# One sink transposition per pair instead of two, and later products of weights and values, in an attention and feed-forward kernel

## The chip, the cores and the metric

The kernel runs on one core of a Trainium2 chip. The metric is the device time of one execution in microseconds (us), as the median of several runs.

## The reference

What is computed is windowed attention with sinks, and behind it a feed-forward part. There are 4 batches, 8 heads, 768 tokens and 64 elements per head; a token sees the first 4 tokens (sinks) and the last 128.

```python
scores = scale * np.matmul(q, k.transpose(0, 1, 3, 2))
keep = is_sink | in_window
scores = np.where(keep, scores, -1000000000.0)
a = np.exp(scores - np.max(scores, axis=-1, keepdims=True))
a = a / (np.sum(a, axis=-1, keepdims=True) + 1e-09)
attn = np.matmul(a, v)                    # heads side by side: 3072 x 512
h = attn @ w_in                           # 512 -> 2048
g = h * np.clip(h + 3.0, 0.0, 6.0) / 6.0
out = g @ w_out                           # 2048 -> 512
```

## The kernel before

**Tiling.** A unit is 256 tokens of one batch (`u` = 0, 1, 2), and a pair is two heads of a unit (`p` = 0 to 3). That makes 48 pairs, listed in `pus`: first the 16 pairs of the four units with `u` = 0, then 32 pairs with `u` > 0, batch by batch. Only the latter have a separate block of sinks (16 key columns), since the first 256 tokens hold the sinks themselves. The first ten pairs are `plain` and use fp32 operands. All others split each operand into a high and a low part (`split_parts`, line 28) in the type fp32r, and multiply the parts.

**Steps of a pair.** `A_kq` and `A_v` load K, Q and V. `B_k` and `B_q` split K and Q, and copy the parts between partitions by DMA (`K`, `Q`, one buffer each). `C_score` computes the scores of one head `h` and one tile `t` of 128 tokens on TensorE, and VectorE adds the mask and finds the minimum (line 314). `C_soft`, after the second tile of a head, runs the exponential on ScalarE (336), the reciprocal on VectorE (339), an addition on GpSimd (344) and the normalization (322). For `u` > 0 and `h` = 1 it then splits the sink weights of both heads and both tiles into `ssc` on VectorE (351 to 354). `D_pt` transposes the weights of a head on TensorE (362), splits them on ScalarE and VectorE into `ph` and `pl`, and GpSimd masks these (380, 382). `D_snk` transposes the sink weights: two products of `ssc` with the identity (392), and one copy to `pz` (395). `E_av` multiplies values and weights of a head into `av` (431); its last product for `u` > 0 takes the split sink values `vs` and `pz`. `E_out`, after head 1, adds the two halves on ScalarE and VectorE (452, 453) and splits the result into `xh` and `xl`.

**Sink values.** `batch_loads` loads them once per batch, at step V of the round in which that batch's first pair with `u` = 1 comes to E: `raw_s` by DMA from `vsx`, then ScalarE and VectorE split it into `vs`. There is one buffer `vs`. It has 128 partitions, of which the load fills 64; GpSimd clears it once, ahead of the first load (195).

**Feed-forward part.** When the fourth pair of a unit has passed `E_av` of head 1, `slot_E` appends the unit's 34 steps to `queues`: 16 of the first layer (`ffn1`, 12 matmuls of 256 columns each, line 469), 16 of the second (`ffn2`, 6 matmuls of 512 columns, line 489), and two outputs (`ffn_out`), which have no matmul. `drain(n)` takes n steps from the queues. A step is held back until enough weights have been loaded; these come with the step W of the first pairs.

**Order.** Instructions are issued in the order that the loop over `s` writes. In round `s`, the string `ORDER` (line 566) names the steps: C and D are for pair `s - 1`, E for pair `s - 2`, B for pair `s`, and V and L load ahead. Each `-` takes one feed-forward step. The framework inserts the semaphores, and it may place an instruction ahead of others that have no buffer yet. All PSUM tiles share 8 banks. The lines that the change touches are 179, 190, 192 to 198, 351, 385 to 396, 427, 566 and the layout of `vsx` at 737.

Of the kernel before, what the change touches and what calls it, by code (L numbers as in the profile page):

```python
# [9 lines left out]
F32 = mybir.dt.float32  # L10
F32R = mybir.dt.float32r
# [7 lines left out]
P = 128  # L19
SK = 16  # L20
# [24 lines left out]
def attn_ffn_kernel(ctx: ExitStack, tc: tile.TileContext, qx, kx, vx, vfx, vsx, n_sink, window, w_in, w_out, out):  # L45
    nc = tc.nc
    B, NU, NP = qx.shape[0:3]
    NT, DM = out.shape
    NFP = w_in.shape[0]
    H, D, UT = 2 * NP, 64, 256  # L50
    S = NU * UT
# [5 lines left out]
    work = fast.enter_context(tc.tile_pool(name="work", bufs=2))  # L57
# [11 lines left out]
    ident_r = const.tile([P, P], F32R, name="ident_r")  # L69
# [45 lines left out]
    def bias_from(dst, keep, engine=nc.vector):  # L115
        engine.tensor_scalar(out=dst, in0=keep, scalar1=-1.0, scalar2=BIG, op0=ALU.add, op1=ALU.mult)
# [15 lines left out]
    def weng(which, at):  # L132
        return {"D": nc.vector, "P": nc.gpsimd, "A": nc.scalar}[which[at % len(which)]]
# [42 lines left out]

    ssc = work.tile([P, 2, P], F32R, name="ssc", bufs=1)
    sinks = {}  # L180

    def later_constants():

        bias_from(m_t0[:, 0:P], prev, nc.gpsimd)
        bias_from(m_t0[:, P:2 * P], own, nc.gpsimd)
        bias_from(m_t0[:, 2 * P:W2], snk[:, 0:SK], nc.gpsimd)
        nc.gpsimd.tensor_copy(out=m_t1[:, 0:P], in_=m_t0[:, 0:P])
        nc.gpsimd.tensor_copy(out=m_t1[:, P:P + SK], in_=m_t0[:, 2 * P:W2])
        nc.gpsimd.tensor_copy(out=m_t1[:, P + SK:W2], in_=m_t0[:, P:2 * P])
        nc.gpsimd.memset(ssc.bitcast(F32), 0.0)  # L190

    def batch_loads(b):
        if not sinks:
            sinks["v"] = work.tile([P, NP, 4 * D], F32R, tag="vs", name="vs", bufs=1)
            nc.gpsimd.memset(sinks["v"].bitcast(F32), 0.0)
        v4 = sinks["v"][0:4 * SK].rearrange("p a (h d) -> p a h d", h=4)
        raw_s = work.tile([P, NP, 2, D], F32, tag="gf", name="raw_s", bufs=2)[0:4 * SK]
        nc.sync.dma_start(out=raw_s, in_=vsx[b])
        split_parts(nc, v4[:, :, 0::2, :], v4[:, :, 1::2, :], raw_s, nc.scalar, nc.vector)

# [127 lines left out]
    def C_soft(s, h):  # L328
        b, u, p = pus[s]
        d = st_[s]  # L330
        nb, sm, rc = d["nb"], d["sm"], d["rc"]
        hs = slice(2 * h, 2 * h + 2)
        live = [(0, W2), (0, W2)] if u else [(0, P), (0, 2 * P)]
        for t in range(2):
            i, blk = 2 * h + t, cell(s, h, t, *live[t])
            d["exp"] = nc.scalar.activation(out=blk, in_=blk, func=AF.Exp, scale=-1.0,  # L336
                                            bias=nb[:, i:i + 1], accum_out=sm[:, i:i + 1])
        nc.vector.tensor_scalar(out=sm[:, hs], in0=sm[:, hs], scalar1=1e-9, scalar2=None, op0=ALU.add)
        nc.vector.reciprocal(out=rc[:, hs], in_=sm[:, hs])  # L339
        if u:  # L340

            both = d["P"][:, h].rearrange("p (t w) -> p t w", t=2)[:, :, P:2 * P]
            prior = d["P"][:, h, 0:2 * WP].rearrange("p (t w) -> p t w", t=2)[:, :, 0:P]
            nc.gpsimd.tensor_tensor(out=both, in0=both, in1=prior, op=ALU.add)  # L344
            live = [(P, W2), (P, W2)]
        for t in range(2):
            i, blk = 2 * h + t, cell(s, h, t, *live[t])
            norm((NORM0 if s < START else NORM)[i], blk, rc[:, i:i + 1])
        if u and h == 1:

            ss = ssc[:, :, 0:4 * SK].rearrange("p t (k h y) -> p t k h y", k=2, h=2)
            snk_in = d["P"][:, :, 2 * P:2 * WP].rearrange(
                "p h (t y) -> p t h y", t=2)[:, :, :, 0:SK]
            split_parts(nc, ss[:, :, 0], ss[:, :, 1], snk_in, weng(SSE, 0), weng(SSE, 1))
# [30 lines left out]
    def D_snk(s):  # L385
        b, u, p = pus[s]
        if not u:
            return
        d = st_[s]
        sp = ps.tile([P, 512], F32, tag="bank", name="spt")  # L390
        for t in range(2):
            nc.tensor.matmul(out=sp[:, t * P:(t + 1) * P], lhsT=ssc[:, t, :],
                             rhs=ident_r, start=True, stop=True)
        pz = work.tile([P, UT], F32R, name="pz", bufs=1)
        nc.scalar.copy(out=pz, in_=sp[:, 0:UT])
        d["pz"] = pz

    def E_av(s, h):
        b, u, p = pus[s]
        d = st_[s]  # L400
        VS = d["VS"]
        if h == 0:
            d["av"] = ps.tile([P, 2, UT], F32, tag="bank", name="av")
            if not plain(s):
                d["tmp"] = work.tile([P, UT], F32, name="tmp", bufs=1)
        acc = d["av"][:, h, :]

        if u:
            ops = [(1, P, 0, UT), (0, 0, 0, P), (2, 3 * P, P, UT)]
        else:  # L410
            ops = [(0, 0, 0, UT), (1, 2 * P, P, UT)]
        if plain(s):
            pf = d[f"pt{h}"]
            seq = [(VS[:, slot, h, :], pf[:, c:c + o1 - o0], d["av"][:, 0, o0:o1]) for slot, c, o0, o1 in ops]
        else:

            ph, pl = d[f"pt{h}"]
            vsl = slice(2 * D * h, 2 * D * (h + 1))
            vhi = slice(2 * D * h, 2 * D * h + D)
            high = [(VS[:, slot, vsl], ph[:, c:c + o1 - o0], acc[:, o0:o1]) for slot, c, o0, o1 in ops]  # L420
            low = [(VS[:, slot, vhi], pl[:, c:c + o1 - o0], acc[0:D, o0:o1]) for slot, c, o0, o1 in ops]
            seq = [high[0]]
            for a, l in zip(high[1:], low[1:]):
                seq += [a, l]

            if u:
                seq += [low[0], (sinks["v"][:, p, vsl], d["pz"], acc)]
            else:
                seq.append((VS[:, 0, vsl], pl[:, 0:UT], acc))
        for j, (l, r, o) in enumerate(seq):  # L430
            nc.tensor.matmul(out=o, lhsT=l, rhs=r, start=(j == 0 and (h == 0 or not plain(s))),  # L431
                             stop=(j == len(seq) - 1 and (h == 1 or not plain(s))))
        if h == 1:
            E_out(s)
# [128 lines left out]
                dsts = [out[r0 + P * tt:r0 + P * (tt + 1), :] for tt in range(2)]  # L563
                queues.append(ffn_steps(units.index((b, u)), xt[(b, u)], work, ps, ps, dsts, "bank"))

    ORDER = "V C00 - C01 E0 - C10 - C11 E1 L - Bk - Bq W - D0 - S D1 -"
    MULT = [1] * 12
    WN = [0, 1, 1, 1, 1, 4, 4, 4, 4, 4, 4, 4]

    for s in range(NS + 2):  # L570
        if s == 3:
            later_constants()
        for step in ORDER.split():
            if step == "-":
# [43 lines left out]
    with tc.If(flag == 1):  # L618
        with ExitStack() as gen:
# [71 lines left out]
            with tc.For_i(0, B, 1) as bi:  # L691
                for u in range(NU):
                    xn = gp.tile([P, NP, UT], F32, name="xn")
                    for c in range(NP):
                        nc.sync.dma_start(out=xn[:, c, :],
                                          in_=xv[ds(bi, 1), :, c, u * UT:(u + 1) * UT].rearrange("o p s -> (o p) s"))
# [12 lines left out]
def _layout(q, k, v, n_sink, window, moe_w_in, moe_w_out):  # L709

    import numpy as _np

    B, H, S, D = q.shape
    NU, NP, T = S // 256, H // 2, 128
    qT = q.reshape(B, NP, 2, S, D).transpose(0, 1, 2, 4, 3).reshape(B, NP, T, S)
    kT = k.reshape(B, NP, 2, S, D).transpose(0, 1, 2, 4, 3).reshape(B, NP, T, S)
    vp = v.reshape(B, NP, 2, S, D).transpose(0, 1, 3, 2, 4)
    qx = _np.zeros((B, NU, NP, T, 256), q.dtype)
    kx = _np.zeros((B, NU, NP, T, 400), k.dtype)
    vx = _np.zeros((B, NU, NP, T, 3, 2, D), v.dtype)  # L720
    for u in range(NU):
        qx[:, u] = qT[..., 256 * u:256 * (u + 1)]
        if u:
            at = [range(256 * u - T, 256 * u + T), range(16), range(256 * u + T, 256 * (u + 1))]
            tiles = range(2 * u - 1, 2 * u + 2)
        else:
            at = [range(256)]
            tiles = range(2)
        at = [j for r in at for j in r]
        kx[:, u, :, :, 0:len(at)] = kT[..., at]  # L730
        for j, t in enumerate(tiles):
            vx[:, u, :, :, j] = vp[:, :, T * t:T * (t + 1)]

    vfx = _np.zeros((B, NP, T, 2, 2, 2, D), v.dtype)
    for h in range(2):
        vfx[:, :, :, :, h, h] = vp[:, :, 0:2 * T, h].reshape(B, NP, 2, T, D).transpose(0, 1, 3, 2, 4)
    vsx = _np.zeros((B, 4, 16, NP, 2, D), v.dtype)
    for r in range(4):
        vsx[:, r, :, :, r % 2] = vp[:, :, 0:16, r % 2].transpose(0, 2, 1, 3)
    DM, DF = moe_w_in.shape  # L740
    w_in = moe_w_in.reshape(DM // T, T, DF // 256, 256).transpose(2, 1, 0, 3)
    w_out = moe_w_out.reshape(DF // 256, 2, T, DM).transpose(0, 2, 1, 3)
    return {'qx': qx, 'kx': kx, 'vx': vx,
            'vfx': vfx.reshape(B, NP, T, 2, 2, 2 * D),
            'vsx': vsx.reshape(B, 64, NP, 2, D), 'n_sink': n_sink, 'window': window, 'w_in': w_in, 'w_out': w_out}


# [24 lines left out]
```

## Time and profile before

| | us |
|---|---|
| median of 3 runs (lowest to highest) | 739.97 (739.43 to 742.04) |
| the profiled execution, its own time | 739.71 |
| its span, first to last instruction | 738.0 |
| TensorE matmuls busy | 715.6 |
| TensorE weight loads busy | 642.3 |
| VectorE busy | 509.2 |
| ScalarE busy | 423.3 |
| GpSimd busy | 172.6 |

The span is the profiled execution from its first to its last instruction. Busy times of an engine are added up over its instructions without overlap. Matmuls are pipelined, so their rows overlap, and TensorE's busy share says little about single ones. In the rows, PE is TensorE's matmul, PEld its weight load, DVE is VectorE, ACT is ScalarE, POOL is GpSimd, and SPq is the queue from which SyncE issues DMAs. L392 is line 392 of the kernel. `out<-in` names the tile written and the tiles read.

### The profile page before, as it was taken

How to read it: one execution, taken by the hardware profiler on the slowest of the kernel's cores; microseconds unless marked ns; L12 is line 12 of the kernel's file. 1: busy time of each engine (PE TensorE's matmuls, PEld its weight loads, DVE VectorE, ACT ScalarE, POOL GpSimd, SP SyncE). 2: the span in 40 equal slices, each digit the busy share in tenths (PEclk: the TensorE clock that was granted, in tenths of full speed). 3: DMA queues.
4: the chain of work that ended last, by engine and by line, in shares of the span. 5: the costliest groups of instructions: out<-in, count | busy, mean ns of one | idle time of the engine just before them, and what ended most of it. 6: DMA issues, size and time to landing. Idle time of an engine off the chain costs nothing.

```text
span 738.0 us, 14278 instructions
## 1 busy us (share of the span) xinstructions
PE 715.6 (97%) x4804; PEld 642.3 (87%) x4804; DVE 509.2 (69%) x1418; ACT 423.3 (57%) x1107; POOL 172.6 (23%) x337
## 2 busy tenths in 40 slices
PE   8899999999999999999999999999999999999996
PEld 7677788999989998989898989899889889998995
DVE  5798999666777767776866876866876775633321
ACT  5998987657556556556555555755655654411111
POOL 1000000000233533433433442343343343200000
PEclk9999999999999999999999999999999999999998
DMA  6657673535536436436435644643643632000000
GB/s 235 185 179 228 197 239 101 144 94 151 132 98 169 117 96 175 126 89 169 118 96 127 158 105 103 171 108 99 175 116 88 168 89 60 30 1 1 30 1 33
DMA packets 55345, 88.58 MB, mean 120 GB/s; under 512 B 8416, under 2 KB 38368, under 8 KB 55264
## 3 DMA queue, kind: packets, MB, share of 16 engines
q1 hardware_dynamic: 55120, 87.59, 43.8%
q8 instruction: 40, 0.66, 0.4%
q14 instruction: 41, 0.34, 0.1%
q10 hardware_dynamic: 144, 0.00, 0.0%
HBM read 41.95 MB, written 6.29 MB: 65 GB/s over the span
## 4 chain that ended last, share of the span: by engine, by line
PE 74%; DVE 8%; ACT 8%; DMA 4%; issue 3%; POOL 2%; SPq 1%; DVEq 0%; ACTq 0%; POOLq 0%
PE o L489 29%; PE hps L469 29%; PE av L431 6%; PE sp L312 4%; PE pt L362 2%; PE sp L307 2%; DMA st<-in_w_out_dram 1%; ACT Pt L336 1%; ACT Pt L322 1%; DMA st<-in_w_in_dram 1%; POOL Pt L344 1%; DVE Pt L314 1%; DVE tmp L453 1%; ACT Ph L336 1%; DVE xl L455 1%
## 5 line engine op out<-in xcount | busy, mean ns | idle before, releaser
L469 PE MATMUL hps<-xh,wih 128*128 128x256 f32 x768 | 220.4, 287 | 2.8 <-ACT wih L35 2.6
L469 PE MATMUL hps<-xh,wil 128*128 128x256 f32 x768 | 217.5, 283 | 0.1
L469 PE MATMUL hps<-xl,wih 128*128 128x256 f32 x768 | 216.3, 282 | 0.0
L489 PE MATMUL o<-woh,gh 128*128 128x512 f32 x384 | 155.7, 405 | 2.1 <-DVE gh L41 1.9
L489 PE MATMUL o<-woh,g 128*128 128x512 f32 x384 | 151.8, 397 | 0.6 <-DVE g L478 0.5
L489 PE MATMUL o<-wol,gh 128*128 128x512 f32 x384 | 151.3, 394 | 0.0
L469 PEld LDWEIGHTS hps<-xh,wih 128*128 128x128 f32 x768 | 144.7, 188 | 5.9 <-ACT wih L35 3.9
L469 PEld LDWEIGHTS hps<-xl,wih 128*128 128x128 f32 x768 | 144.7, 188 | 1.4
L469 PEld LDWEIGHTS hps<-xh,wil 128*128 128x128 f32 x768 | 144.5, 188 | 1.6 <-DVE wil L165 0.5
L336 ACT ACTIVATE Pt<-Pt,nb 128x272 f32<-128x272 f32 (+2 forms) x152 | 77.1, 508 | 73.4 <-DVE nb L314 71.8
L475 ACT ACTIVATE gf<-hps,three 128x512 f32<-128x512 f32 x96 | 65.8, 685 | 83.9 <-PE hps L469 83.0
L476 DVE SCALAR_TENSOR_TENSOR gf<-gf,hps 128x512 f32<-128x512 f32 x96 | 65.9, 686 | 67.3 <-ACT gf L475 66.3
L344 POOL TENSOR_TENSOR Pt<-Pt 128x256 f32<-128x256 f32 x64 | 47.9, 748 | 194.1 <-ACT Pt L336 194.1
L489 PEld LDWEIGHTS o<-woh,g 128*128 128x128 f32 x384 | 72.2, 188 | 19.7 <-DVE g L478 3.0
L322 ACT ACTIVATE Pt<-Pt,rc 128x144 f32<-128x144 f32 (+2 forms) x152 | 55.8, 415 | 54.0 <-DVE rc L339 32.4
L489 PEld LDWEIGHTS o<-woh,gh 128*128 128x128 f32 x384 | 72.3, 188 | 13.0 <-DVE gh L41 2.8
L314 DVE CUSTOM_DVE_ANT_0 Pt<-sp,m_t 128x272 f32<-128x272 f32 x128 | 54.5, 434 | 41.9 <-PE sp L312 41.8
L489 PEld LDWEIGHTS o<-wol,gh 128*128 128x128 f32 x384 | 72.5, 189 | 10.5
L478 DVE TENSOR_TENSOR g<-gf,gh 128x512 fp32r<-128x512 f32 x96 | 70.0, 729 | 1.2
L312 PE MATMUL sp<-K,Q 128*128 128x272 f32 (+2 forms) x304 | 61.0, 286 | 0.2 <-issue 0.2
L312 PEld LDWEIGHTS sp<-K,Q 128*128 128x128 f32 x304 | 51.3, 188 | 7.0 <-DMA Q<-qt 0.4
L380 POOL TENSOR_SCALAR_AFFINE_SELECT ph<-ph 128x256 fp32r<-128x256 f32 x64 | 29.8, 466 | 113.7 <-ACT ph L35 113.2
(97 smaller groups left out, 1111.2 us busy)
## 6 DMA issues: line engine op xcount, KB each, us to landing
K<-kt SPq DMA_DIRECT2D x128, 200.0 KB, 3.5
Q<-qt SPq DMA_DIRECT2D x152, 64.0 KB, 2.5
st<-in_w_in_dram SPq DMA_DIRECT2D x16, 512.0 KB, 4.3
st<-in_w_out_dram SPq DMA_DIRECT2D x16, 512.0 KB, 5.3
kr<-in_kx_dram SPq DMA_DIRECT2D x32, 200.0 KB, 2.5
qr<-in_qx_dram SPq DMA_DIRECT2D x48, 128.0 KB, 2.4
out_dram<-ost SPq DMA_DIRECT2D x24, 256.0 KB, 2.5
vr<-in_vx_dram SPq DMA_DIRECT2D x32, 192.0 KB, 2.6
```

Of the source, the lines that this page charges most:

```text
L312: nc.tensor.matmul(out=sp[:, 0:w], lhsT=Q[:, h, t * P:(t + 1) * P], rhs=K[:, h, part, k0c:k0c + w], start=(part == 0), stop=(part == 1))
L314: d["min"] = nc.vector.tensor_tensor_reduce(out=cell(s, h, t, 0, w), in0=sp[:, 0:w], in1=m[:, 0:w], scale=-SCALE, scalar=3.0e38, op0=ALU.a ...
L322: nc.scalar.mul(out=blk, in_=blk, mul=c)
L336: d["exp"] = nc.scalar.activation(out=blk, in_=blk, func=AF.Exp, scale=-1.0, bias=nb[:, i:i + 1], accum_out=sm[:, i:i + 1])
L344: nc.gpsimd.tensor_tensor(out=both, in0=both, in1=prior, op=ALU.add)
L380: nc.gpsimd.affine_select(out=prior[i], in_=own[i], pattern=[[0, 2], [-1, P]], base=0, channel_multiplier=1, compare_op=ALU.is_gt, fill=0.0)
L431: nc.tensor.matmul(out=o, lhsT=l, rhs=r, start=(j == 0 and (h == 0 or not plain(s))), stop=(j == len(seq) - 1 and (h == 1 or not plain(s))))
L469: nc.tensor.matmul(out=hp[:, half, :], lhsT=l, rhs=r, start=(j == 0), stop=(j == n - 1))
L475: nc.scalar.activation(out=gf, in_=hp, func=AF.Relu, bias=three, scale=1.0)
L476: nc.vector.scalar_tensor_tensor(out=gf, in0=gf, scalar=6.0, in1=hp, op0=ALU.min, op1=ALU.mult)
L478: eng(GLO, state["n"] * NP).tensor_tensor(out=g, in0=gf, in1=gh.bitcast(F32), op=ALU.subtract)
L489: nc.tensor.matmul(out=acc, lhsT=l[:, f, ts_], rhs=r[i][:, f, :], start=(i == 0 and f == 0 and j == 0), stop=(i == NFP - 1 and f == 1 and ...
```

## The change

`ssc` gets one tile of 128 columns, in which the parts, tiles and heads of the sink weights lie side by side, so one product with the identity transposes them all. Its result has the rows of tile 0 in partitions 0 to 63 and those of tile 1 in partitions 64 to 127. Two copies put the first into columns 0 to 127 of `pz`, and the second into columns 128 to 255; the rest of `pz` was cleared once and stays zero. `pz` is now one lasting tile. The sink values are laid out twice, in all 128 partitions, and `vs` isn't cleared any more. In `ORDER`, E0 moves from behind C01 to behind C11, E1 moves from behind C11 to behind Bk, and S moves behind D1. There are eight `-` in both orders.

```diff
-    ssc = work.tile([P, 2, P], F32R, name="ssc", bufs=1)
+    ssc = work.tile([P, P], F32R, name="ssc", bufs=1)
+    pz = work.tile([P, UT], F32R, name="pz", bufs=1)
...
-        nc.gpsimd.memset(ssc.bitcast(F32), 0.0)
+        nc.gpsimd.memset(pz.bitcast(F32), 0.0)
...
             sinks["v"] = work.tile([P, NP, 4 * D], F32R, tag="vs", name="vs", bufs=1)
-            nc.gpsimd.memset(sinks["v"].bitcast(F32), 0.0)
-        v4 = sinks["v"][0:4 * SK].rearrange("p a (h d) -> p a h d", h=4)
-        raw_s = work.tile([P, NP, 2, D], F32, tag="gf", name="raw_s", bufs=2)[0:4 * SK]
+        v4 = sinks["v"].rearrange("p a (h d) -> p a h d", h=4)
+        raw_s = work.tile([P, NP, 2, D], F32, tag="gf", name="raw_s", bufs=2)
...
-            ss = ssc[:, :, 0:4 * SK].rearrange("p t (k h y) -> p t k h y", k=2, h=2)
+            ss = ssc.rearrange("p (t k h y) -> p t k h y", t=2, k=2, h=2)
...
         sp = ps.tile([P, 512], F32, tag="bank", name="spt")
+        nc.tensor.matmul(out=sp[:, 0:P], lhsT=ssc, rhs=ident_r, start=True, stop=True)
         for t in range(2):
-            nc.tensor.matmul(out=sp[:, t * P:(t + 1) * P], lhsT=ssc[:, t, :],
-                             rhs=ident_r, start=True, stop=True)
-        pz = work.tile([P, UT], F32R, name="pz", bufs=1)
-        nc.scalar.copy(out=pz, in_=sp[:, 0:UT])
-        d["pz"] = pz
+            rows = slice(4 * SK * t, 4 * SK * (t + 1))
+            nc.scalar.copy(out=pz[rows, t * P:(t + 1) * P], in_=sp[rows, 0:P])
...
-                seq += [low[0], (sinks["v"][:, p, vsl], d["pz"], acc)]
+                seq += [low[0], (sinks["v"][:, p, vsl], pz, acc)]
...
-    ORDER = "V C00 - C01 E0 - C10 - C11 E1 L - Bk - Bq W - D0 - S D1 -"
+    ORDER = "V C00 - C01 - C10 - C11 E0 L - Bk E1 - Bq W - D0 - D1 S -"
...
-    vsx = _np.zeros((B, 4, 16, NP, 2, D), v.dtype)
-    for r in range(4):
+    vsx = _np.zeros((B, 8, 16, NP, 2, D), v.dtype)
+    for r in range(8):
         vsx[:, r, :, :, r % 2] = vp[:, :, 0:16, r % 2].transpose(0, 2, 1, 3)
```

## Rows read from the trace of the kernel before

**Rows 1.** The page: busy us (share of the span) and instructions.

```profile
PE 715.6 (97%) x4804; PEld 642.3 (87%) x4804; DVE 509.2 (69%) x1418; ACT 423.3 (57%) x1107; POOL 172.6 (23%) x337
```

**Rows 2.** Stretches: length, busy us (instructions) by engine, granted clock, DMA share, GB/s.

```profile
0.00:120.00 120.00, 112.13 (x670) 91.69 (x670) 100.23 (x298) 101.95 (x251) 3.09 (x16) 1.00 0.67 207
120.00:640.00 520.00, 512.23 (x3550) 468.16 (x3551) 378.01 (x1069) 306.63 (x834) 169.55 (x321) 1.00 0.46 119
```

**Rows 3.** Waits, 120 to 640 us: waiting line, releaser, us, times, longest.

```profile
PE av L431 <- DVE vs L30: 3.2, 4, 1.5
PE spt L392 <- DVE ssc L30: 1.6, 2, 1.2
PE o L489 <- DVE gh L41: 1.1, 1, 1.1
...
PE o L489 <- DVE g L478: 0.5, 1, 0.5
...
PEld av L431 <- DVE vs L30: 4.2, 4, 1.7
```

**Rows 4.** Line 392: minimum/median/maximum ns, first and last start in us.

```profile
L392 PEld LDWEIGHTS spt<-ident_r,ssc x64: 186/188/192, 199.5 to 633.8; 128*128 128x128 f32 x64
L392 PE MATMUL spt<-ident_r,ssc x64: 221/273/327, 199.7 to 633.8; 128*128 128x128 f32 x64
```

**Rows 5.** Chain of waits, 250 to 260 us: start, us, engine, tile, line, count.

```profile
251.88 1.43 PE hps L469 x12
...
254.97 0.17 PE spt L392 x2
255.14 0.25 PE pt L362 x2
255.39 1.40 PE o L489 x6
...
258.42 0.25 PE sp L312 x2
258.67 0.65 PE av L431 x7
```

**Rows 6.** Timeline at the fourth batch's sink values: start, us; idle before in brackets.

```profile
533.69 0.49 SPq L198 DMA_DIRECT2D raw_s<-in_vsx_dram  x1
...
538.25 0.85 DVE L30 TENSOR_TENSOR vs<-raw_s,vs 64x512 fp32r<-64x512 f32 x1 [1.26 <-ACT vs L35]
...
539.16 0.38 PE L431 MATMUL av<-pz,vs 128*128 128x256 f32 x1 [0.87 <-DVE vs L30]
```

**Rows 7.** DMA issues: count, KB each, median us to landing.

```profile
VF<-in_vfx_dram SPq DMA_DIRECT2D x10, 256.0 KB, 3.8
...
raw_s<-in_vsx_dram SPq DMA_DIRECT2D x4, 128.0 KB, 2.8
```

**Rows 8.** Groups by form, ScalarE: busy us, mean ns, idle before.

```profile
L452 ACT COPY tmp<-av 64x256 f32<-64x256 f32 x76 | 27.8, 366 | 23.5 <-DVE tmp L453 13.2 <-DVE xl L455 9.0
...
L395 ACT CAST pz<-spt 128x256 fp32r<-128x256 f32 x32 | 11.7, 366 | 4.0 <-PE spt L392 4.0
...
L336 ACT ACTIVATE Ph<-Ph,nb 128x256 f32<-128x256 f32 x20 | 10.0, 498 | 0.0
...
L336 ACT ACTIVATE Ph<-Ph,nb 128x128 f32<-128x128 f32 x20 | 7.9, 394 | 7.3 <-DVE nb L314 7.2
```

**Rows 9.** Waits of TensorE, 0 to 120 us.

```profile
PE pt L362 <- DVE Ph L324: 2.4, 3, 1.1
```

**Rows 10.** Timeline around 265 us, SP and TensorE; last row, Q's issues, us to landing.

```profile
265.15 3.02 SPq L275 DMA_DIRECT2D Q<-qt  x4
...
270.82 0.41 PE L312 MATMUL sp<-K,Q 128*128 128x272 f32 x2
...
Q<-qt SPq DMA_DIRECT2D x152, 64.0 KB, 2.5
```

**Rows 11.** Groups by form, VectorE, line 453.

```profile
L453 DVE TENSOR_TENSOR tmp<-av,tmp 64x256 f32<-64x256 f32 x76 | 31.9, 420 | 16.2 <-ACT tmp L452 15.7
```

More of the change, by code (lines that the diff above doesn't have):

```diff
@@ L744, in _layout @@
             'vfx': vfx.reshape(B, NP, T, 2, 2, 2 * D),
-            'vsx': vsx.reshape(B, 64, NP, 2, D), 'n_sink': n_sink, 'window': window, 'w_in': w_in, 'w_out': w_out}
+            'vsx': vsx.reshape(B, 128, NP, 2, D), 'n_sink': n_sink, 'window': window, 'w_in': w_in, 'w_out': w_out}
 def kernel(**inputs):
```

## Prediction

> **What bounds the kernel now.** I read the share of busy time first: TensorE's matmuls cover 97% of the span, its weight loads 87% [rows 1]. Such a share is an average, so I cut the span into stretches [rows 2]. Up to 120 us, while weights are loaded and the first tiles (plain fp32) run, VectorE and ScalarE are busy for 100.2 and 102.0 of 120 us and TensorE for 112.1. From 120 to 640 us, where the 32 pairs with sinks lie (sink transpositions from 199.5 to 633.8 us [rows 4]), TensorE is busy for 512.2 of 520 us, VectorE for 378.0 and ScalarE for 306.6. After 640 us only the feed-forward part is left. The granted clock is 1.00, 2.4 GHz, in the first two stretches. So between 120 and 640 us a matmul taken away is worth its place in the stream, and a wait of TensorE is worth its length; work of the other engines is free as long as it ends in time.
>
> Then I read whom TensorE waits for in that stretch [rows 3]: 3.2 us for `vs`, the split sink values (four waits, one per batch), 1.6 us for `ssc` (two), 1.6 us for `gh` and `g` of the feed-forward part. That is 6.4 of the 7.8 us by which TensorE falls short of 520.
>
> A matmul's own duration is no price, since matmuls overlap (the sink transpositions show a median of 273 ns [rows 4]). The price is what the chain of waits gives to a run of them [rows 5]: 12 feed-forward matmuls of 256 columns in 1.43 us, 119 ns each; two sink transpositions in 0.17 us, 85 ns each.
>
> **The sum, part by part.** *One transposition fewer.* Now each sink pair issues two 128x128 products with the identity, x64 [rows 4]; then one, x32. Each is worth 0.17/2 = 0.085 us; bounds are half of a 256-column slot, 0.06, and half of the 0.25 us that the two transpositions of D1 take behind them [rows 5], 0.12. I take 0.085, the row of the thing itself: 32 x 0.085 = 2.7 us (1.9 to 3.8). The Trainium skill, page "TensorE: Matmul & The Clock Gate", section "Wait — 56ns, not 53.3ns?", has a 128-column matmul at 55.6 ns in a warm stream; by it this term would be 1.8 us, an estimate from that page, and the sum 0.9 us smaller. The row is of the same instruction with its own weight load and decides.
>
> *Products of weights and values later.* E0 goes past C10, C11 and two feed-forward steps, E1 past the loads of the next pair (L), one step and Bk. Their last product reads `vs`, which is filled anew per batch. In the fourth batch the load is issued at 533.69, VectorE ends the split at 538.25 + 0.85 = 539.10, and the product starts at 539.16, 0.87 us late [rows 6]. In the new order it comes two steps (1.4 us each, as the 12 matmuls or the six wide ones of the second layer [rows 5]) and two scores (0.25 each, of two matmuls [rows 5]) later: 3.3 us. The longest wait [rows 3] is 1.5, so all four go. Worth: 3.2 us as TensorE's idle, 4.2 as the idle of its weight loads [rows 3]; I take 3.2 plus 4 x 0.1 for the product after the stall (0.38 against its usual 0.28 us), 3.6. What is late next is nothing of `vs`.
>
> *Sink rows doubled.* The load grows from 64 rows (128 KB) to 128 rows (256 KB). Rows at both ends: 2.8 us to land for 128 KB, 3.8 for the 256 KB of VF [rows 7], so up to 1.0 us more, four times; the nearest row in size is VF and I take the full 1.0. It is covered by the 3.3 - 1.5 = 1.8 us that are left; uncovered it would cost 4 us at most. The split keeps 512 elements per row, and a row count doesn't show in these durations: `tmp` with 64 rows of 256 takes as long as `pz` with 128 [rows 8]. GpSimd's clearing of `vs` goes; the clearing of `pz` replaces that of `ssc` (256 columns both). Neither is waited for.
>
> *Two copies for `pz` instead of one.* Now 128x256 in 0.366 us. No row shows 64x128. From below: 256 against 128 columns differ by 0.104 us for the exponentials [rows 8], so 0.26 each, 0.16 more per pair; from above: two full ones, 0.37 more. I take 0.16, since columns and not rows set it: 32 x 0.16 = 5 us of ScalarE, 12 at most, in a stretch where it has 213 us free [rows 2]. The copies now stand behind the evacuation of D1 on ScalarE, which that gains. Their reader is E0's last product, four steps later. Uncovered, it would be 0.16 per pair on the path. VectorE's split into `ssc` has the same 128x64 elements: nothing.
>
> *S behind D1, C11 ahead of E0.* Two pairs waited for `ssc`. C11 now runs 0.65 us (seven products of E0 [rows 5]) earlier and S 0.25 later, but D1 comes first and needs the normalized weights, ready 0.4 us before `ssc` (two VectorE splits). I take half of the 1.6 us, 0.8 (bounds 0 and 1.6).
>
> *First stretch.* Three waits of the transpositions for VectorE's normalizing, 2.4 us together [rows 9]; with C11 ahead of E0 they may shrink. But VectorE and ScalarE are 84% busy there [rows 2], converting weights. I take 0 (bounds 0 and 2.4). The feed-forward steps of the first unit begin one step later; they are held back by the count of loaded weights anyway.
>
> *Queues.* E issues no DMA, so SP's queue keeps its order. ScalarE's split of V waits for the buffer that E1 of two pairs before reads, now about 2 us later; its own reader comes two pairs later, so nothing. SP's K and Q copies of the next pair overwrite what C11 reads, so they go out behind it. In one pair Q's four go from 265.15 to 268.17, behind K's, land 2.5 us later at 270.7, and the next score starts at 270.82 [rows 10]. There is little room; but between C11 and the next pair's C00 there were five steps and one E, and will be five steps and two E, 0.65 us more. I cost this at nothing; 0.5 us late in each pair would be 16 us.
>
> Sum: 2.7 + 3.6 + 0.8 = 7.1 us. The profiled execution took 739.71 us (span 738.0 and 1.7 around it), 0.26 below the median: 739.97 - 7.1 = 732.9.
>
> **Rivals.** *The waits only move (0.15).* `vs` is ready in time, but TensorE, no longer stopped, meets the next late thing. For: 0.2 to 1.1 us waits for `gh`, `g` and `ssc` are there already [rows 3]. Against: VectorE has 27% free in this stretch [rows 2]. Then only the matmul pays: 739.7 - 2.7 = 737.0.
>
> *TensorE isn't the bound (0.08).* The Trainium skill, page "Perfetto Trace Analysis", section "Identifying the Most-Contended Engine", says to judge TensorE's headroom by weight loads, not by matmul busy time. As a mechanism here: the 13% without a weight load [rows 1] would be real room, the stream would be held by buffers or evacuations, and what is saved would turn into other gaps; the time stays 739.7. Against: six 512-column matmuls take 1.40 us, 233 ns each, back to back, while a weight load is 188 ns [rows 4, 5], so weight loads rest there with the array full.
>
> *Slower: VectorE's second half fills up (0.07).* E_out's VectorE operations (two sums of 0.42 us each [rows 11] and the two parts of x) move behind Bk, into the half pair that already has the splits of K, V, Q and of both D's. The feed-forward chain (gf, gh, g) queues behind them, and the second-layer product waits for `gh` or `g`, as it does once with 1.1 us [rows 3]. It decides from 7.1/32 = 0.22 us of new wait per pair; at 0.5 us it is 16 us against 7: 739.7 - 7.1 + 16 = 748.6. Against: VectorE is busy 73% [rows 2], and E_out ran into that half before too, a step and an E (2 us) earlier.
>
> **How the numbers follow.** Forecast 0.70, rivals 0.15, 0.08, 0.07. The likeliest gives 732.8. Its own ends: all low, 1.9 + 3.2 + 0 = 5.1, gives 734.9; all high, 3.8 + 4.2 + 1.6 + 2.4 = 12.0, gives 728.0. The range reaches to the first rival with 1.5 us beyond and leaves out the slower one: 728.5 to 738.5. About 0.5%, 3.7 us, is what a measurement can tell from no change, so faster means below 736.3: the forecast and a quarter of the first rival, 0.74; same 0.19; slower 0.07.
>
> **What would show it.** Right: x32 sink transpositions; TensorE's row for `vs` gone; TensorE idle from 120 to 640 us below 4 us; pz copies x64 near 0.26 us; K and Q landing before their scores. Wrong: a row of TensorE for `gh`, `g`, `pz` or Q of several us, an unchanged or larger idle sum, or a first stretch that takes longer.

## The result and the profile after

The changed kernel takes 731.26 us (median of 4 runs, 730.63 to 732.62) against 739.76 for the kernel before in the same job: a ratio of 0.988, 95% interval 0.986 to 0.990, 8.5 us less. The forecast was 732.8 us, range 728.5 to 738.5. The profiled execution took 730.63 us, span 728.9, which is 9.1 less than the span before.

The page and the stretches of the changed kernel, columns as in [rows 1, 2]:

```profile
PE 709.6 (97%) x4772; PEld 635.8 (87%) x4772; DVE 495.4 (68%) x1418; ACT 426.3 (58%) x1139; POOL 169.6 (23%) x336
```

```profile
0.00:120.00 120.00, 111.15 (x684) 91.76 (x685) 103.25 (x301) 104.56 (x257) 3.08 (x16) 1.00 0.66 210
120.00:640.00 520.00, 515.60 (x3571) 469.67 (x3570) 366.09 (x1075) 309.71 (x864) 166.54 (x320) 1.00 0.47 121
```

There are 32 matmuls fewer. From 120 to 640 us TensorE falls short by 4.4 us instead of 7.8 [rows 2]. In the first 120 us it has issued 684 matmuls instead of 670. Its waits from 120 to 640 us in the changed kernel are these (compare [rows 3]):

```profile
PE sp L312 <- DMA Q<-qt: 1.9, 3, 1.0
PE o L487 <- DVE gh L41: 1.4, 4, 0.5
PE o L487 <- DVE g L476: 0.4, 2, 0.2
```

The rows for `vs` and `ssc`, 4.8 us, are gone. A row for Q has come, 1.9 us. The instructions of `ssc`, `pz` and the sink values in the changed kernel (minimum/median/maximum ns, first and last start), and the DMA issues (columns as in [rows 7]):

```profile
L391 PE MATMUL spt<-ident_r,ssc x32: 305/306/308, 197.6 to 622.8; 128*128 128x128 f32 x32
...
L394 ACT CAST pz<-spt x64: 246/260/267, 198.2 to 623.6; 64x128 fp32r<-64x128 f32 x64
...
L35 ACT ACTIVATE vs<-raw_s x4: 615/634/635, 201.5 to 527.8; 128x512 fp32r<-128x512 f32 x4
```

```profile
VF<-in_vfx_dram SPq DMA_DIRECT2D x10, 256.0 KB, 3.6
...
raw_s<-in_vsx_dram SPq DMA_DIRECT2D x4, 256.0 KB, 2.9
```

A copy into half of `pz` takes 0.260 us. Twice the sink values land in 2.9 us, against 2.8 before [rows 7].

The chain of waits of the changed kernel around a sink transposition, columns as in [rows 5]:

```profile
250.36 1.43 PE hps L467 x12
251.79 0.22 PE pt L362 x2
252.01 0.06 PE spt L391
252.07 1.47 PE hps L467 x12
...
258.50 0.25 PE sp L312 x2
...
267.67 0.25 PE sp L312 x2
```

Before, the two sink products and D1's two transpositions took 0.17 + 0.25 = 0.42 us together [rows 5]. Now it is 0.22 + 0.06, and 0.04 more for the run behind them (1.47 us instead of 1.43): 0.32. So by this one pair a sink transposition is worth 0.10 us, and 32 of them 3.2 us.

### The profile page after: what moved, and what is told of

Read it like the earlier page. It is cut to its first block, busy times and chain, and to the rows that moved or that the text cites. A ratio compares the mean times of both kernels' runs of the same rounds, so it can differ in the third digit from the quotient of the medians.

```text
span 728.9 us, 14295 instructions
## 1 busy us (share of the span) xinstructions
PE 709.6 (97%) x4772; PEld 635.8 (87%) x4772; DVE 495.4 (68%) x1418; ACT 426.3 (58%) x1139; POOL 169.6 (23%) x336
## 4 chain that ended last, share of the span: by engine, by line
PE 79%; DVE 7%; ACT 5%; DMA 5%; issue 2%; SPq 1%; POOL 0%; ACTq 0%; DVEq 0%; POOLq 0%
PE hps L467 32%; PE o L487 31%; PE av L429 6%; PE sp L312 5%; PE pt L362 3%; DMA K<-kt 2%; PE sp L307 2%; SPq L262 1%; DMA Q<-qt 1%; DVE gf L474 1%; DVE g L476 1%; ACT Pt L336 1%; DMA st<-in_w_out_dram 1%; ACT gf L473 1%; PE idle L81 1%
## 5 line engine op out<-in xcount | busy, mean ns | idle before, releaser
L380 POOL TENSOR_SCALAR_AFFINE_SELECT ph<-ph 128x256 fp32r<-128x256 f32 x64 | 32.5, 512 | 155.7 <-ACT ph L35 155.7
```

The lines of the kernel that those rows point to most:

```text
L380: nc.gpsimd.affine_select(out=prior[i], in_=own[i], pattern=[[0, 2], [-1, P]], base=0, channel_multiplier=1, compare_op=ALU.is_gt, fill=0.0)
```

## The experiments

Each ratio is to the kernel before, run on the same chip in the same job, with a 95% interval. Three more measures come from the profiled execution, one of each kernel, without an interval. **The rest** runs from the issue of the first output DMA to the end of the span. It compares kernels of one order alone, because the first output stands at different places of TensorE's stream: behind 726 or 727 matmuls in the order of before (before, e1, e4, e8), 743 or 744 in the new one, 731 or 732 with E1 behind E0 in the first rounds (e6, e9, e12). **The middle** runs from the first score product of the first pair with sinks to that of the last pair. It holds the same steps of the pairs in every kernel, 31 of the 32 sink transpositions and all four waits for `vs`. **The end** is what follows. The two executions of the changed kernel agree in the middle to 0.02 us (424.75 and 424.77), those of e6 and e12 to 0.03.

| kernel | median us | ratio (interval) | first output at | the rest | the middle | the end |
|---|---|---|---|---|---|---|
| before | | 1 | 129.8 | 608.2 | 433.6 | 116.6 |
| changed | 731.26 | 0.988 (0.986 to 0.990) | 130.4 | 598.5 | 424.8 | 118.6 |
| e1 merge only | 738.02 | 0.995 (0.994 to 0.997) | 132.2 | 605.3 | 430.9 | 116.6 |
| e2 order only | 737.78 | 0.996 (0.994 to 0.998) | 132.6 | 602.5 | 428.5 | 118.9 |
| e3 second product | 734.97 | 0.991 (0.989 to 0.993) | 132.7 | 602.7 | 428.4 | 119.1 |
| e4 sinks once | 735.96 | 0.994 (0.992 to 0.996) | 130.0 | 604.3 | 429.7 | 116.6 |
| e5 S ahead of D1 | 730.39 | 0.987 (0.984 to 0.990) | 129.9 | 598.2 | 424.1 | 119.0 |
| e6 E1 behind E0 | 726.87 | 0.981 (0.979 to 0.983) | 126.4 | 598.1 | 424.3 | 116.7 |
| e7 output on ScalarE | 735.73 | 0.992 (0.989 to 0.994) | 136.7 | 603.1 | 429.4 | 117.7 |
| e8 first rounds old | 732.98 | 0.989 (0.987 to 0.992) | 130.7 | 601.4 | 426.6 | 116.7 |
| e9 E1 early in first rounds | 728.68 | 0.984 (0.982 to 0.987) | 127.5 | 599.3 | 426.2 | 116.0 |
| e10 E1 early in later rounds | 735.70 | 0.992 (0.989 to 0.994) | 129.6 | 603.7 | 429.6 | 118.8 |
| e11 changed again | 731.07 | 0.986 (0.984 to 0.989) | 129.9 | 598.5 | 424.8 | 118.5 |
| e12 E1 behind E0 again | 727.19 | 0.981 (0.978 to 0.983) | 128.6 | 598.0 | 424.4 | 116.6 |

The stretch ahead of the middle, the middle and the end, of the kernel before and then of the changed one, and behind them the middles of e2 and e3, columns as in [rows 2]; each middle goes from the start of one `sp` product to that of another:

```profile
0.00:187.80 187.80, 179.53 (x1128) 153.32 (x1129) 148.89 (x441) 145.70 (x369) 4.05 (x17) 1.00 0.59 175
187.80:621.39 433.59, 426.22 (x2971) 389.67 (x2969) 316.77 (x885) 254.60 (x693) 162.05 (x307) 1.00 0.49 124
621.39:738.00 116.61, 109.89 (x709) 99.30 (x707) 43.49 (x93) 23.02 (x45) 6.54 (x14) 0.98 0.04 15
```

```profile
0.00:185.56 185.56, 175.85 (x1117) 150.09 (x1117) 148.95 (x440) 145.39 (x369) 3.08 (x16) 1.00 0.59 176
185.56:610.31 424.75, 421.55 (x2945) 385.24 (x2943) 303.09 (x886) 257.19 (x724) 160.89 (x308) 1.00 0.50 129
610.31:728.90 118.59, 112.20 (x715) 100.48 (x713) 43.31 (x93) 23.73 (x47) 5.65 (x13) 1.00 0.04 15
```

```profile
187.75:616.22 428.47, 425.17 (x2976) 389.47 (x2974) 302.14 (x886) 249.48 (x692) 161.54 (x309) 1.00 0.49 126
187.90:616.26 428.36, 424.76 (x2975) 388.64 (x2974) 301.78 (x886) 254.20 (x723) 161.71 (x309) 1.00 0.50 127
```

**The merge alone (e1).** The changed kernel with the order of before:

```diff
-    ORDER = "V C00 - C01 - C10 - C11 E0 L - Bk E1 - Bq W - D0 - D1 S -"
+    ORDER = "V C00 - C01 E0 - C10 - C11 E1 L - Bk - Bq W - D0 - S D1 -"
```

> The changed kernel with the order of steps of before: one sink transposition, two copies for pz, sink values in 128 rows, E0 and S where they were. My theory: only the matmul term is earned, 32 x 0.085 = 2.7 us (up to 3.8), and the four waits of TensorE for vs stay (3 us or more): 736 to 737 us. Rival, the order is needed for nothing: 731.3 as the whole change. Rival, TensorE isn't the bound: 739.8, as before. If the doubled load of sink values made itself felt, the waits for vs would grow by up to 1.0 us each, and the time would be up to 4 us more, 740 to 741.

738.02 us, 0.995, or 3.5 us less (2.2 to 4.7); the rest is 2.9 us shorter, the middle 2.7. TensorE's waits from 120 to 640 us, first three rows:

```profile
PE av L429 <- DVE vs L30: 3.6, 4, 1.4
PE o L487 <- DVE gh L41: 1.5, 2, 1.2
PE spt L391 <- DVE ssc L30: 1.3, 2, 0.7
```

The matmul is earned, and the waits for `vs` stay, as the theory said. The doubled load lengthens them from 3.2 to 3.6 us, not by 1.0 us each.

**The order alone (e2).** The kernel before with the new `ORDER`:

> The kernel before with the new order of steps alone: two sink transpositions, one copy, sink values in 64 rows. My theory: the waits for vs go (3.6 us), those for ssc shrink or go (0.8 to 1.6), so 734.5 to 735.5 us, and TensorE's row for vs is empty. Rival, the waits only move: 739.8, with new rows for gh, g or Q of as many us. If the two parts are independent, the gains of this run and of the run with the order of before add up to the 8.5 us of the whole.

737.78 us, 3.2 us less (1.6 to 4.7): the sign is right, the size of the median below the forecast. TensorE's waits from 120 to 640 us have no row for `vs` or `ssc`:

```profile
PE o L489 <- DVE gh L41: 1.9, 4, 0.7
PE sp L312 <- DMA Q<-qt: 1.4, 2, 0.8
PE o L489 <- DVE g L478: 0.2, 1, 0.2
```

The middle is 5.1 us shorter; the forecast for these waits was 4.4. The end is 2.3 us longer (see E1 below). Most of the scatter goes with the clock. Four of e2's twelve executions had a mean granted clock of 0.997 or more and took 734.5 to 735.7 us, about as forecast; seven at 0.990 to 0.994 took 737.3 to 740.9. The kernel before took 739.1 to 741.6 us in twelve executions at 0.998 or 0.999, and 742.0 to 744.1 in nine at 0.993 or 0.994. In the profiled execution of e2 the clock fell in the first stretch, at a wait of 2.2 us for a weight:

```profile
60.00:65.00 5.00, 2.79 (x14) 2.13 (x12) 4.20 (x14) 4.37 (x13) 0.00 (x0) 0.90 0.41 118
65.00:70.00 5.00, 5.00 (x24) 3.81 (x23) 4.45 (x13) 4.46 (x10) 0.00 (x0) 0.76 0.70 233
```

With e1 the two parts give 3.5 + 3.2 = 6.7 us by the runs, against 8.5 to 8.8 for the whole, and 2.7 + 5.1 = 7.8 against 8.8 by the middle. Within the intervals the parts add up. The missing 1.0 us is about what TensorE's waits grew in e1 (8.9 us without a matmul from 120 to 640 us, against 7.8).

**The price of a transposition (e3).**

```diff
         nc.tensor.matmul(out=sp[:, 0:P], lhsT=ssc, rhs=ident_r, start=True, stop=True)
+        nc.tensor.matmul(out=sp[:, P:2 * P], lhsT=ssc, rhs=ident_r, start=True, stop=True)
```

> The changed kernel with one more 128x128 product of ssc and the identity per pair with sinks, into columns of the bank that nobody reads. It measures the price of one transposition: by the chain of waits 0.085 to 0.10 us, 32 of them 2.7 to 3.2 us, so 734.0 to 734.5; by 55.6 ns a matmul 1.8 us, so 733.1; if TensorE isn't the bound, 731.3.

734.97 us. By the ratios, 0.9912 against 0.9881, it costs 0.0031 of 740, 2.3 us, but the two intervals overlap; by the rest it costs 4.2. By the middle it costs 3.6 us, 428.4 against 424.8, for the 31 products in it; the clock was 1.00 in both. The order alone (e2), which differs from the changed kernel by the merge, gives 3.7 the same way. That is 0.12 us a product and 3.8 us for 32, and it excludes both 0.06 us and that TensorE isn't the bound.

**The price of the waits for `vs` (e4).** The kernel before, with one load of sink values instead of four:

```diff
-                if 2 <= s and pus[s - 2][1:] == (1, 0):
-                    batch_loads(pus[s - 2][0])
+                if s == 17:
+                    batch_loads(0)
```

> The kernel before with the sink values loaded and split once, for the first batch, one round earlier; the three later loads and splits are left out, so the later batches use the first one's sink values. All four waits for vs are gone, and nothing else is changed. My theory: 3.6 us less, 736.2 (3.2 to 4.2 us less). Rival, the waits only move: 739.0 to 739.8. The left-out loads and splits are 3 x 0.6 us of ScalarE and 3 x 0.8 us of VectorE, which have room there.

735.96 us, 4.7 us less (3.2 to 6.2); the rest and the middle are 3.9 us shorter. TensorE's busy time from 120 to 640 us rises by 2.8 us against [rows 2]:

```profile
120.00:640.00 520.00, 515.05 (x3581) 471.71 (x3581) 378.50 (x1072) 306.85 (x835) 166.59 (x321) 1.00 0.46 119
```

So what TensorE waited for `vs`, 3.2 us, came back: 2.8 us as busy time, 3.9 by the middle. Its other waits grew by 0.4 us, from 4.0 to 4.4.

**The place of S (e5).** The changed kernel with `... D0 - S D1 -`:

> The changed kernel with S back ahead of D1; E0 and E1 stay late. My theory: the waits for vs stay away, and S, with C11 0.65 us earlier, waits for ssc for at most 1.6 us in all, so 731.3 to 733.0, and a row of TensorE for ssc may come back. Rival, the place of S is what makes the order pay: 734 or more.

730.39 us, as the changed kernel within the interval, and with no row for `ssc`. The place of S makes no difference that shows. What ended the waits for `ssc` is then, by elimination, C11 ahead of E0; in e6, which has this and E1 back behind E0, 0.2 of the 1.6 us is left.

**The place of E1 (e6, e12, e11).** The changed kernel with E0 late and E1 right behind it; e12 repeats it beside e11, the changed kernel, on one chip:

```diff
-    ORDER = "V C00 - C01 - C10 - C11 E0 L - Bk E1 - Bq W - D0 - D1 S -"
+    ORDER = "V C00 - C01 - C10 - C11 E0 E1 L - Bk - Bq W - D0 - D1 S -"
```

> The changed kernel with E1 where it was, behind E0 and ahead of L, so that only E0 is late. My theory: vs is needed first by E0, so all of the gain comes from E0's place: 731.3, within 1 us. Rival, the later E1 counts too, by the time it gives GpSimd's masks or by what it moves on VectorE: 733 to 735, with waits of TensorE for ph or pl. Second rival, E1 and E_out behind Bk load VectorE in the second half and cost waits for gh and g (1.8 us in the changed kernel's trace): 730.

> The changed kernel as it is, as the measure for the others on this chip: 0.988 of the kernel before (0.986 to 0.990).

> The order with E1 behind E0 throughout, beside the changed kernel on one chip. If the 5 us are real: 0.981 of the kernel before and 0.993 of the changed one. If they came from the chip or from scatter: as the changed kernel.

726.87 us, and 727.19 beside 731.07: 4 us less than the changed kernel, on one chip, with intervals that don't touch (0.978 to 0.983 against 0.984 to 0.989). None of the three theories had this. The middle is 0.4 us shorter, and no row for Q is left in it. The end is 1.9 us shorter (116.7 and 116.6 against 118.6 and 118.5). The first unit's feed-forward steps begin one step earlier: ahead of the middle e6 has issued 1129 matmuls, as the kernel before (1128), and the changed kernel 1117. The step that is missing there is left for the end. What remains of the 4 us lies ahead of the middle, where executions scatter: it begins at 183.47 (e6) and 185.64 (e12) instead of 185.56 and 185.10 (e11). The first output leaves at 126.4 and 128.6 us instead of 130.4 and 129.9, but behind 12 matmuls fewer. The rows of `ost` (ns, first and last issue), of the changed kernel and then of e6:

```profile
L494 SPq DMA_DIRECT2D out_dram<-ost x24: 332/370/1659, 130.4 to 723.6; - x24
```

```profile
L494 SPq DMA_DIRECT2D out_dram<-ost x24: 332/350/608, 126.4 to 718.5; - x24
```

**Where E1's place counts (e9, e10).** The order with E1 behind E0 in rounds 0 to 15 alone (e9), and from round 16 on alone (e10). The same edit, with `FIRST` and `ORDER` exchanged:

```diff
-        for step in ORDER.split():
+        for step in (FIRST if s < 16 else ORDER).split():
```

> The changed kernel with E1 behind E0 (ahead of L) in rounds 0 to 15 and in its changed place, behind Bk, from round 16 on. The run with E1 behind E0 throughout took 0.981 of the kernel before, the changed kernel 0.988: 5 us between them. Theory: these are won in the first stretch, where the first unit's feed-forward steps begin one step earlier and the last weights are issued at 105.5 instead of 107.2 us. Then this one takes as long as that run, 727 to 728 us (0.981 to 0.983), and the first output leaves near 126.4 us. Rival: they are won later, where the masks and VectorE's second half have room; then 731 (0.988).

> The mirror of the run before: E1 behind Bk in rounds 0 to 15 and behind E0 from round 16 on. By the theory that the first stretch pays, 730 to 731.5 (0.987 to 0.989), with the first output near 130 us; by the rival, 727 (0.981).

e9 takes 728.68 us, 2.4 of the 3.9 us less than e11, and its first output leaves at 127.5. Its interval overlaps those of e11 and e12, so the runs alone don't settle the share. The profile agrees with the theory in part: the end is 2.5 us shorter than in e11, but the middle is about 1.5 us longer. e10 misses: 735.7 us instead of 730 to 731.5. Its first output leaves at 129.6, as forecast, and the end is as in the changed kernel, but the middle is 4.8 us longer. TensorE's waits of e10 from 120 to 640 us:

```profile
PE o L487 <- DVE gh L41: 4.6, 4, 2.0
PE sp L312 <- DMA Q<-qt: 1.5, 2, 0.9
```

The longest of these, 2.0 us, was at 526 us, and with it the clock fell, which cost about 1.7 us (an estimate, 0.34 of 5 us):

```profile
525.00:530.00 5.00, 3.64 (x10) 2.88 (x11) 3.95 (x8) 1.63 (x4) 1.41 (x3) 0.66 0.51 147
```

So the same later order gives a middle of 424.3 us (e6, e12) and of 429.6 us (e10), after different first rounds; and the changed kernel's later order gives 424.8 us, or 426.2 (e9) and 426.6 (e8). What differs is which feed-forward step falls at which place of a round: a unit's 34 steps are spread over rounds of 8, and a first unit that starts one step later shifts all that follow. That this shift is the cause is my reading; no run moved it alone.

**The first rounds in the order of before (e8).** As e9, with the order of before as `FIRST`.

> The changed kernel with the order of before in rounds 0 to 15 and the new order from round 16 on. In the traces of the new order, TensorE waits 2.2 to 2.3 us once for a weight conversion and 2.2 us for gh in the first 120 us, and the first output leaves at 130.4 to 132.7 us, against 129.8 to 132.2 with the order of before. Theory, the new order costs 1 to 2 us in the first stretch: 729.3 to 730.3. Rival, that is the scatter of single executions: 731.3.

732.98 us, no gain. The theory that the new order costs time in the first stretch falls. The middle is 1.8 us longer than in the changed kernel, so not all of the difference lies there. The last weights are issued at 110.9 us in e8, 109.9 in the kernel before, and 107.2 and 106.1 in the two profiles of the changed kernel. The rows of line 149, before, changed and e8 in turn (ns, first and last issue):

```profile
L149 SPq DMA_DIRECT2D st<-in_w_out_dram x16: 327/328/430, 6.0 to 109.9; - x16
```

```profile
L149 SPq DMA_DIRECT2D st<-in_w_out_dram x16: 327/328/430, 5.9 to 107.2; - x16
```

```profile
L149 SPq DMA_DIRECT2D st<-in_w_out_dram x16: 327/328/430, 5.9 to 110.9; - x16
```

The new order brings the weights 2.7 to 3.8 us earlier. It is E0's move that does it: with E0 behind C11 and a clock of 1.00 in that stretch they come at 105.5 to 107.2 us wherever E1 stands (the changed kernel twice, e5, e6, e9, e10, e12), with the order of before at 109.9 to 110.9 (before, e1, e4, e8). TensorE's wait for VectorE's normalizing in that stretch falls from 2.4 us [rows 9] to 0.6:

```profile
PE pt L362 <- DVE Ph L324: 0.6, 1, 0.6
```

**Outputs from another queue (e7).**

```diff
-        nc.sync.dma_start(out=dst, in_=o)
+        nc.scalar.dma_start(out=dst, in_=o)
```

> The changed kernel with the 24 output DMAs issued by ScalarE instead of SP. In the changed kernel TensorE waited for Q three times, 1.9 us in all, and in two of them (1.03 and 0.65 us) an output DMA had stood on SP's queue between K's copies and Q's, waiting for ScalarE. My theory: those two waits go, 1.0 to 1.7 us, 729.6 to 730.3; one of 0.26 us stays. Rival, Q is late for another reason, or ScalarE's issuing costs as much: 731.3 or more.

735.73 us, a miss, and slower than the changed kernel. A part of that goes with the clock: its six executions had mean granted clocks of 0.990 to 0.999, and at like clocks they are 0.7 to 2.7 us slower than those of the changed kernel (731.91 us at 0.999 against 730.09 to 731.18, 734.39 at 0.997 against 731.70 and 732.62). The profiled one is the slowest, at 0.990. The wait for Q didn't go; it has grown to 3.5 us in two places. SP's queue at the longest wait, in the changed kernel and then in e7 (start, us of issuing):

```profile
396.70 2.44 SPq L262 DMA_DIRECT2D K<-kt  x4
399.24 0.80 SPq L494 DMA_DIRECT2D out_dram<-ost  x1
400.09 2.82 SPq L275 DMA_DIRECT2D Q<-qt  x4
```

```profile
405.17 2.55 SPq L262 DMA_DIRECT2D K<-kt  x4
407.82 4.44 SPq L275 DMA_DIRECT2D Q<-qt  x4
```

Without the output in between, issuing Q took 4.44 us instead of 2.82, and Q came no sooner. The output's place on SP's queue isn't the cause by itself. In the two longest of the three waits (1.03 and 0.65 us) the two steps without matmuls (a unit's outputs) fall between C11 and the next C00; in the third (0.26 us) one does. In the changed kernel C11 ran at 396.25 and Q was waited for from 402.7, 6.5 us later, instead of 258.50 to 267.67, 9.2 us, in an ordinary pair. In e6 and e12, where every feed-forward step falls one place earlier, TensorE has no row for Q.

## Why the prediction was right, step by step

**The bound.** Right. A product more (e3), a wait less (e4) and both parts of the change (e1, e2) each move the time the way TensorE's stream says. The rule of the Trainium skill, page "Perfetto Trace Analysis", section "Identifying the Most-Contended Engine", goes by the busy share of weight loads (and by the share of peak throughput, which was not worked out here); taken by weight loads alone it would have put the headroom at the 13% without one. That share is still 87% busy in the changed kernel while the span is 9.1 us shorter. For the larger part the 13% stand for the wide products: at 233 ns a product and 188 ns a weight load, 1152 of them leave about 52 of 93 us without a weight load (an estimate).

**One transposition fewer, 2.7 us.** Too small: 3.8 by the middle (e3, and e2 against the changed kernel), at the upper bound of 1.9 to 3.8. Half of the 0.17 us of the two sink products wasn't the price; half of what D1's two transpositions take, 0.12, was. The chain of one pair gave 3.2, e1 3.5 (2.2 to 4.7). The Trainium skill, page "TensorE: Matmul & The Clock Gate", section "Wait — 56ns, not 53.3ns?", would give 1.8 us, an estimate from its 55.6 ns. The measured 0.12 us a product decides against it.

**`vs`, 3.6 us.** Right: 4.7 (3.2 to 6.2) by the ratio of e4, 3.9 by its middle, with 0.4 us more of other waits.

**Sink rows doubled.** Hidden, as forecast, but the size was wrong: I took the VF row, 1.0 us more, and the load took 0.1 us more. The nearest row in size was not the nearest in kind.

**Two copies.** 0.260 us each, as estimated; ScalarE stays at 310 of 520 us.

**`ssc`, 0.8 us.** All 1.6 us went; the order without the merge shortens the middle by 5.1 us, 1.2 more than the waits for `vs` alone (e4). The reason was C11's earlier place; S behind D1, which I counted in, does nothing that shows (e5).

**Queues, nothing.** This step failed in part. The 0.65 us that I found hold for an ordinary pair: from C11 to the next C00 it is 9.2 us now against 8.6 before. I reckoned with five steps of 1.4 us and left out that two of a unit's 34 have no matmul. Where both fall into that gap, Q is late: 1.7 of the 1.9 us.

**First stretch, nothing.** Nearly right in the sum, by luck, since two errors cancel. C11 ahead of E0 brings the weights 2.7 us earlier and the middle begins 2.2 us earlier (2.7 in e11), which I had only as the upper bound of 2.4. And "held back by the count of loaded weights anyway" was wrong: E1's new place does delay the first unit, by one step, and this step is left for the end, which takes 2.0 us longer. With E1 behind E0 the end takes as long as before (e6, e12).

By the rows of the two profiled executions the 9.1 us are 8.8 in the middle, 2.2 ahead of it, and 2.0 lost at the end. The middle's 8.8 are 5.1 for the order (e2), Q's waits already taken off, and 3.7 for the merge. The forecast had 4.4, 2.7 and nothing at either end, 7.1 in all: the mechanism held, and both terms were too small. (739.97 - 7.1 is 732.87, so the 732.8 is 732.9.) Two of the signs of being right did not come: TensorE's idle from 120 to 640 us is 4.4 us and not below 4, and Q landed late for three scores.

**The rivals.** The waits didn't just move (e4). VectorE's second half didn't fill up in the changed kernel (`gh` and `g` 1.8 us against 1.6). With E1 back behind E0 these waits are 2.6 and 2.5 us (e6, e12) and not shorter. The 4.6 us for `gh` in e10 can't be this rival's, since there E1 is back behind E0 from round 16 on.

**A version that beats both.** E1 right behind E0, with all else as changed: 0.981 of the kernel before (727 us), twice measured.

## What to carry to other kernels

When the bound engine waits once per batch for a reload, moving the reader behind other work is worth the wait in full, if the engine has such work in its stream. Price each moved step on its own and in each stretch: here one half of a move (E0) paid and the other (E1) took part of it back, because it started the feed-forward steps one step later and left that step for the end. Compare stretches that hold the same work: from the first output on, two orders didn't. In a stream with filler steps look at the pairs in which the filler is empty, for there the margins of queues are the smallest.

## What the runs showed that was not expected

The first stretch differs between executions and kernels more than the middle: the first output left between 126.4 and 136.7 us. A part of that is the order, a part TensorE's clock. Stretches of e7, and then of the changed kernel, columns as in [rows 2]:

```profile
60.00:65.00 5.00, 2.07 (x10) 1.37 (x9) 3.31 (x12) 4.40 (x13) 0.00 (x0) 1.00 0.32 88
65.00:70.00 5.00, 5.00 (x21) 3.67 (x21) 4.89 (x12) 4.52 (x9) 0.00 (x0) 0.60 0.67 191
70.00:75.00 5.00, 5.00 (x20) 4.17 (x19) 2.01 (x9) 1.03 (x5) 0.00 (x0) 0.50 0.80 262
75.00:80.00 5.00, 4.02 (x19) 3.34 (x18) 3.63 (x11) 4.46 (x12) 0.00 (x0) 0.88 0.19 61
```

```profile
60.00:65.00 5.00, 2.73 (x14) 1.91 (x14) 4.02 (x14) 4.59 (x14) 0.00 (x0) 1.00 0.45 136
65.00:70.00 5.00, 5.00 (x32) 3.98 (x33) 4.90 (x13) 4.76 (x11) 0.00 (x0) 1.00 0.63 215
```

In e7 TensorE waited 2.9 us for VectorE's conversion of a weight and was busy for 2.07 of 5 us; behind that the granted clock was 0.60, 0.50 and 0.88, where 0.50 is the lower level, 1.2 GHz. In the changed kernel the same wait was 2.3 us, with 2.73 of 5 us busy, and the clock stayed at 1.00; in e2 a wait of 2.2 us, with 2.79 busy, came with 0.90 and 0.76. So no length of wait tells the two apart here. From 65 to 70 us e7 issued 21 matmuls at 0.60 and the changed kernel 32 at 1.00. The clock cost e7 about 5 us there (an estimate, 0.40, 0.50 and 0.12 of 5 us each). The middle is still 4.6 us longer in e7 than in the changed kernel. About 1.7 us of that is a second fall of the clock (an estimate as above), behind the longest wait for Q (2.1 us), and this wait itself is 1.0 us longer than the changed kernel's:

```profile
410.00:415.00 5.00, 2.94 (x22) 2.76 (x21) 4.60 (x11) 3.94 (x12) 3.66 (x8) 0.91 0.66 189
415.00:420.00 5.00, 5.00 (x29) 4.74 (x28) 3.09 (x10) 2.47 (x9) 0.74 (x2) 0.74 0.23 66
```

A copy of 64 rows and 128 columns took 0.260 us and one of 128 rows and 256 columns 0.366 [rows 8], so halving the columns saves 0.106 us, as for the exponentials (0.104).
